# Attention scores as four 64x64 tiles in two PSUM banks, v windows copied by GpSimd, and a new split of PSUM banks

## The chip, the cores and the metric

The kernel runs on one NeuronCore of one Trainium2 chip. Its time is device microseconds (us) of one execution, and the comparison is between medians of several runs. PE is TensorE (PEld its weight loads), DVE is VectorE, ACT is ScalarE, POOL is GpSimd, and SP is the engine that issues most DMAs.

## What is computed

The reference is sliding-window attention over 64 keys, followed by two mixture-of-experts layers. The change touches only the attention:

```python
q, k, v: [4, 8, 576, 64] float32           # batch, heads, positions, head dim
scores = (1.0 / np.sqrt(64)) * np.matmul(q, k.transpose(0, 1, 3, 2))
rel = pos[:, None] - pos[None, :]
scores = np.where((rel >= 0) & (rel < 64), scores, -1000000000.0)
scores = scores - np.max(scores, axis=-1, keepdims=True)
attn = np.exp(scores)
attn = attn / (np.sum(attn, axis=-1, keepdims=True) + 1e-09)
out = np.matmul(attn, v)                   # then [2304, 512] tokens
x = _moe_ref(x=out, ...)                   # 8 experts, 288 tokens each
return _moe2_ref(x=x, ...)                 # 8 experts, argmax of a softmax
```

## The kernel before

The 2304 tokens are cut into 18 tiles `t` of 128 tokens. A tile holds two blocks of 64 queries (`bb` = 0, 1). A block needs 128 keys: its own 64 and the 64 before them. The 8 heads are worked on as two halves `hf` = 0, 1: the even heads lie on partitions 0 to 63 of the transposed q and k, the odd ones on 64 to 127.

For one tile the work runs as follows. `load_qk` and `load_v` bring q, k and v by DMA from SP. `tr` transposes k and q on TensorE into a PSUM tile `tr`, and VectorE or ScalarE copies them to `K1` and `qa`. `attn(t, hf)` writes a mask into the PSUM tile `S` by an identity matmul (L377) and adds the scores of four heads onto it (L380: for each head two matmuls of 64x64 weights, one for each block). VectorE takes the row maximum (`mx`, L387) and its negative multiple (`nb`, L388). ScalarE makes the exponentials `P` (L392). TensorE transposes `P` into the PSUM tile `PT` (L398), and VectorE or ScalarE copies that to `pt`. TensorE multiplies by v into the PSUM tile `PV` (L408; the 65th column of v is one, and gives the sum). `fin` normalizes on VectorE into `x` (`sm`, its reciprocal and a product: L442, L444, L445). Then `parts` splits x into two f16 halves `x16` (high part on ScalarE, VectorE or GpSimd; low part L415 on GpSimd), stores them to `xd` by DMA, and transposes them (`xT`, L429); they are copied to `xt`, and the gate's logits follow (L470, L472, reduced by VectorE into `LG`, L475).

The second matmul operand of PV is v of the window: `vs` is v of the tile, and `vw` has the first 64 rows of this tile and the last 64 rows of the tile before. `windows` fills `vw` by two DMAs a tile from SP (L344, L347).

A planner sets the order in which each engine's instructions stand (`_Order`): every step is added with its engine or engines, an assumed duration, the tiles that it reads and writes, and a priority; `emit` places steps in assumed time and issues them in that order. A tile with n buffers can be written again when the steps of n tiles before are done. PSUM has 8 banks, and the attention shares them as tr 1, xT 1, S 2, PT 2, PV 2:

```python
bufs = dict(lk=4, lq=4, vs=4, vw=4, tr=1, xT=1, qa=3, S=2, mx=4, nb=4, P=3, PT=2, pt=3,
            PV=2, sm=4, x=3, x16=3, xt=3, K=RS)
```

When the last tile's logits are there, the attention's buffers are given back, and only then do the loads of the expert weights (L183) and the routing begin; the experts' matmuls follow to the end of the program.

Of the kernel before, what the change touches and what calls it, by code (L numbers as in the profile page):

```python
# [21 lines left out]
BF = mybir.dt.bfloat16  # L22
I32 = mybir.dt.int32
AF = mybir.ActivationFunctionType
ALU = mybir.AluOpType
# [118 lines left out]
def attn_moe_moe(ctx: ExitStack, tc: tile.TileContext, q, k, v, w_gate, w1a, w2a, emb, tau, w1b, w2b, out, dbg=None):  # L144
    nc = tc.nc
    dbg = dbg or {}
    B, H, S, D = q.shape
# [65 lines left out]
    idb = consts.tile([128, 128], BF, name="idb")  # L213
# [45 lines left out]
    MV = -8.0e9  # L259
    pa = ExitStack()  # L260
    wk = pa.enter_context(tc.tile_pool(name="attn", bufs=2))
    ps = pa.enter_context(tc.tile_pool(name="attn_ps", bufs=2, space=PSUM))
    dk = wk.tile([128, 2, 64], I32, name="dk", bufs=1)
    for g in range(2):
        nc.gpsimd.iota(dk[64 * g:64 * g + 64], pattern=[[0, 2], [1, 64]], base=0, channel_multiplier=-1)
    mt = wk.tile([128, 2, 64], F32, name="mt", bufs=1)
    masks = [wk.tile([128, 4, 2, 64], BF, name=f"mask{i}", bufs=1) for i in range(3)]
    for bb in range(2):
        sl = slice(64 * bb, 64 * bb + 64)
        nc.vector.tensor_scalar(mt[sl, bb], dk[sl, bb], 0.0, MV, op0=ALU.is_gt, op1=ALU.mult)  # L270
        nc.vector.tensor_scalar(mt[sl, 1 - bb], dk[sl, 1 - bb], 0.0, MV, op0=ALU.is_le, op1=ALU.mult)
    for i in range(3):
        nc.vector.tensor_copy(masks[i], mt[:, None].to_broadcast([128, 4, 2, 64]))
    nc.vector.memset(masks[1][0:64, :, 1], MV)
    nc.vector.memset(masks[2][64:128, :, 0], MV)
    wgf = wk.tile([128, NC, E], F32, name="wgf", bufs=1)
    nc.scalar.dma_start(wgf, w_gate.rearrange("(c p) e -> p c e", p=128))
    wgc = wk.tile([128, NC, 2, E], F16, name="wgc", bufs=1)
# [3 lines left out]
    RS = 4  # L282
# [1 line left out]
    K1 = wk.tile([128, RS, 4, 2, 64], F32, name="K1", bufs=1)  # L284
    nc.gpsimd.memset(K1[:, RS - 1, :, 1], 0.0)

    bufs = dict(lk=4, lq=4, vs=4, vw=4, tr=1, xT=1, qa=3, S=2, mx=4, nb=4, P=3, PT=2, pt=3,
                PV=2, sm=4, x=3, x16=3, xt=3, K=RS)
    shapes = dict(lk=([128, 8, 64], F32), lq=([128, 8, 64], F32), vs=([128, 8, 65], F32),
                  vw=([128, 8, 65], F32), qa=([128, 4, 2, 64], F32), S=([128, 4, 128], F32),  # L290
                  mx=([128, 4], F32), nb=([128, 4], F32), P=([128, 4, 128], F32), PT=([128, 4, 128], F32),
# [10 lines left out]
    g = g_  # L302
# [7 lines left out]
    def win(h, te, to):  # L310
        a = K1[64 * (h % 2):64 * (h % 2) + 64, te, h // 2]
        ap = [list(z) for z in a.ap]
        ap[1][0] += (to - te) * 512
        return bass.AP(tensor=a.tensor, offset=a.offset, ap=ap)

    TK, LGS = {}, {}
# [24 lines left out]

    def windows(t):
        vs, vw = TK['vs', t], TK['vw', t]
        ls.dma(1.3, .46, lambda: nc.sync.dma_start(g(vw)[0:64], g(vs)[0:64]), (vs,), (vw,), 2 * t)  # L344
        if t + 1 < NT:
            vn = TK['vw', t + 1]
            ls.dma(1.3, .46, lambda: nc.sync.dma_start(g(vn)[64:128], g(vs)[64:128]), (vs,), (vn,), 2 * t + 1)  # L347

    def tr(t, nm, tag='tr'):
        x, p, pr = TK[nm, t], ls.slot(tag), 2 * t - 2  # L350

        def pf():
            return g(p) if tag in ('tr', 'xT') else g(p).rearrange("p a n -> p (a n)")

        def f():
            for n in range(4):
                nc.tensor.transpose(pf()[:, n * 128:(n + 1) * 128], g(x)[:, 2 * n:2 * n + 2].rearrange("p a d -> p (a d)"), idf)
        ls.add('PE', .52 if t else .9, f, (x,), (p,), pr)
        y = TK[nm.upper(), t] = ls.slot('K' if nm == 'k' else 'qa')

        def to():
            z = K1[:, t % RS] if nm == 'k' else g(y)
            return z.rearrange("p h o i -> p (h o i)")
        ls.add(('DVE', 'ACT'), (.68, .6), lambda e: copy(e, to(), pf()), (p,), (y,), pr)

    def attn(t, hf):
        pr = 2 * t + hf
        mk = masks[0]
        if t * 128 % S == 0:
            mk = masks[1]  # L370
        if (t * 128 + 64) % S == 0:
            mk = masks[2]
        p, qa = ls.slot('S'), TK['Q', t]
        te, tp = t % RS, (t - 1) % RS

        def f():
            nc.tensor.matmul(g(p), idb, mk, start=True, stop=True)  # L377
            for hh in range(4):
                for bb in range(2):
                    nc.tensor.matmul(g(p)[bb * 64:bb * 64 + 64, hh],  # L380
                                     g(qa)[64 * hf:64 * hf + 64, hh, bb],
                                     win(2 * hh + hf, te, te if bb else tp), start=False, stop=True,
                                     skip_group_check=True)
        kd = [TK['K', t]] + ([TK['K', t - 1]] if t else [])
        ls.add('PE', 1.2, f, [qa] + kd, (p,), pr)
        mx, nb, P = ls.slot('mx'), ls.slot('nb'), ls.slot('P')
        ls.add('DVE', .68, lambda: nc.vector.tensor_reduce(g(mx), g(p), axis=AX.X, op=ALU.max), (p,), (mx,), pr)  # L387
        ls.add('DVE', .15, lambda: nc.vector.tensor_scalar(g(nb), g(mx), -0.125, None, op0=ALU.mult), (mx,), (nb,), pr)  # L388
# [202 lines left out]
    for t in range(NT):  # L591
        if t + 3 < NT:
            loads(t + 3)
        windows(t)
        attn(t, 0)
        if t + 1 < NT:
            front(t + 1)
        attn(t, 1)
        fin(t)
        if t == 9:  # L600
            small()
        if t == NP:
            spread()
# [706 lines left out]
    for i in range(2):  # L1310
# [5 lines left out]
        def f(i=i, pf=pf):  # L1316
            for l in range(2):
                for c in range(NC):
                    nc.tensor.transpose(pf()[:, l, c], G2[0, i].bitcast(F16)[:, (l * NC + c) * 128:(l * NC + c + 1) * 128], idh)
# [197 lines left out]
```

## Time and profile before

| | |
|---|---|
| median of 3 runs | 677.07 us (674.95 to 679.09) |
| the profiled execution, its own time | 676.5 us |
| its span in the profile | 674.7 us |
| TensorE busy over the span | 615.6 us (91%) |
| VectorE, ScalarE, GpSimd busy | 387.1 us, 325.9 us, 158.5 us |
| mean granted TensorE clock | 0.97 |

The span is what the profiler saw of one execution; the execution's own time is 1.8 us longer. The busy times are sums over stages that have different limits: attention ends after about a fifth of the span, and the experts take the rest.

### The profile page before, as it was taken

What the parts mean: (1) busy time and instruction counts of PE and PEld (TensorE: products, weight loads), DVE (VectorE), ACT (ScalarE), POOL (GpSimd) and SP (SyncE); (2) the same over time, 40 slices, a digit from 0 to 9 for tenths busy, and PEclk for the clock granted to TensorE, in tenths of its full rate; (3) what the DMA queues carried; (4) which work ended last, traced back from release to release, by engine and by line L of the source; (5) the groups of instructions that cost most, each with busy time, mean ns of one, the idle gap of its engine ahead of it and who ended that gap; (6) DMA issues with size and microseconds to landing.
All of it is one profiled execution on the core that took longest, in us unless ns stands there. A gap on an engine that the chain in (4) does not pass through costs nothing. (4 is left out here: it accounts for less than half of the span.)

```text
span 674.7 us, 16654 instructions
## 1 busy us (share of the span) xinstructions
PE 615.6 (91%) x6626; PEld 461.5 (68%) x6644; DVE 387.1 (57%) x995; ACT 325.9 (48%) x626; POOL 158.5 (23%) x222
## 2 busy tenths in 40 slices
PE   7998999878689999999999997898999799899994
PEld 5876787633347887877877887585866577568671
DVE  4777777768702478788688785462656671152010
ACT  3655655556632356556456664362656562352110
POOL 1242122100141243242322110431322430312101
PEclk9999999969989999999999997998999899999997
DMA  9999784154427489999999673496579882132100
GB/s 194 210 238 209 190 203 106 48 204 168 144 61 208 83 243 236 271 276 252 249 279 213 217 247 102 129 365 229 154 279 352 302 307 75 59 104 65 38 22 23
DMA packets 135069, 124.06 MB, mean 184 GB/s; under 512 B 99095, under 2 KB 99223, under 8 KB 134946
## 3 DMA queue, kind: packets, MB, share of 16 engines
q1 hardware_dynamic: 126114, 102.24, 54.4%
q0 software_dynamic: 5616, 17.60, 8.7%
q10 hardware_dynamic: 3216, 2.64, 1.4%
q8 instruction: 69, 1.13, 0.7%
q14 instruction: 54, 0.44, 0.2%
HBM read 94.17 MB, written 14.64 MB: 161 GB/s over the span
## 5 line engine op out<-in xcount | busy, mean ns | idle before, releaser
L1380 PE MATMUL pp<-x,w1h 128*128 128x128 f16 (+1 forms) x1280 | 99.3, 215 | 3.3 <-issue 2.6
L1380 PE MATMUL pp<-x,w1l 128*128 128x128 f16 (+1 forms) x640 | 98.1, 215 | 0.0
L1019 PE MATMUL pp<-xt,w1h 128*128 128x288 f16 x512 | 96.4, 289 | 1.7 <-ACT xt L999 1.7
L1034 PE MATMUL pp<-h,w2h 128*128 128x288 f16 x512 | 94.7, 286 | 0.0
L1380 PEld LDWEIGHTS <-w1h 128*128 128x128 f16 x1280 | 90.6, 100 | 4.4 <-issue 3.0
L1393 PEld LDWEIGHTS <-h 128*128 128x128 f16 (+1 forms) x480 | 47.3, 101 | 53.2 <-issue 1.7
L193 ACT ACTIVATE w2h<-wst 128x1024 f16<-128x1024 f32 x64 | 66.9, 1052 | 17.2 <-DMA wst<-in_moe_w_dram 16.9
L196 DVE SCALAR_TENSOR_TENSOR w2l<-wst,w2h 128x1024 f16<-128x1024 f32 x56 | 67.6, 1219 | 11.3 <-ACT w2h L193 9.9
L1019 PE MATMUL pp<-xt,w1l 128*128 128x288 f16 x256 | 74.0, 289 | 0.0
L1034 PE MATMUL pp<-h,w2l 128*128 128x288 f16 x256 | 73.2, 286 | 0.0
L193 ACT ACTIVATE w1h<-wst 128x1024 f16<-128x1024 f32 x64 | 66.6, 1051 | 13.4 <-DMA wst<-in_moe_w_dram 13.2
L196 DVE SCALAR_TENSOR_TENSOR w1l<-wst,w1h 128x1024 f16<-128x1024 f32 x56 | 67.3, 1214 | 3.3 <-ACT w1h L193 3.1
L1384 DVE SCALAR_TENSOR_TENSOR h<-pp,h 128x512 f16<-128x512 f32 (+1 forms) x40 | 24.8, 620 | 69.8 <-ACT h L1383 69.8
L1380 PEld LDWEIGHTS <-w1l 128*128 128x128 f16 x640 | 62.3, 100 | 0.7 <-issue 0.7
L1019 PEld LDWEIGHTS <-w1h 128*128 128x128 f16 x512 | 49.7, 99 | 14.3 <-issue 1.8
L1034 PEld LDWEIGHTS <-w2h 128*128 128x128 f16 x512 | 49.8, 98 | 12.3
L1393 PE MATMUL pp<-w2h,h 128*128 128x512 f16 (+1 forms) x192 | 57.2, 379 | 0.0
L1397 POOL DMA_INDIRECT out_dram<-o,xg x20 | 19.9, 997 | 147.7 <-ACT o L1396 113.1
L1022 ACT ACTIVATE h<-pp 128x288 f16<-128x288 f32 x64 | 26.2, 409 | 43.9 <-PE pp L1019 41.0
L392 ACT ACTIVATE P<-S,nb 128x128 f32<-128x128 f32 x144 | 41.0, 374 | 11.5 <-DVE sm L444 4.3
L380 PE MATMUL S<-K,qa 64*64 64x128 f32 x576 | 41.4, 285 | 4.9 <-issue 1.8
L1383 ACT ACTIVATE h<-pp 128x512 f16<-128x512 f32 (+1 forms) x40 | 21.7, 542 | 49.5 <-PE pp L1380 44.3
(289 smaller groups left out, 1173.4 us busy)
## 6 DMA issues: line engine op xcount, KB each, us to landing
wst<-in_moe_w_dram SPq DMA_DIRECT2D x124, 512.0 KB, 5.9
yd<-yr SPq DMA_DIRECT2D x8, 578.2 KB, 6.2
xd<-x SPq DMA_DIRECT2D x18, 256.0 KB, 3.1
vw<-vs SPq DMA_DIRECT2D x35, 130.0 KB, 3.8
lk<-in_k_dram SPq DMA_DIRECT2D x16, 256.0 KB, 4.0
lq<-in_q_dram SPq DMA_DIRECT2D x16, 256.0 KB, 4.5
vs<-in_v_dram SPq DMA_DIRECT2D x16, 256.0 KB, 4.9
wst<-in_moe_w_dram ACTq DMA_DIRECT2D x4, 512.0 KB, 5.6
```

Source lines behind the costliest of these rows:

```text
L193: nc.scalar.activation(w_slice(key, i, 0), ST[key, i], AF.Copy, scale=32.0)
L196: nc.vector.scalar_tensor_tensor(w_slice(key, i, 1), ST[key, i], 32.0, w_slice(key, i, 0), op0=ALU.mult, op1=ALU.subtract)
L380: nc.tensor.matmul(g(p)[bb * 64:bb * 64 + 64, hh], g(qa)[64 * hf:64 * hf + 64, hh, bb], win(2 * hh + hf, te, te if bb else tp), start=Fals ...
L392: nc.scalar.activation(g(P)[:, hh], g(p)[:, hh], AF.Exp, bias=g(nb)[:, hh:hh + 1], scale=0.125)
L1019: nc.tensor.matmul(g(p)[:, :CAP], w1s(key, i, c, f_), g(xt)[:, j, c], start=(n == 0), stop=(n == 11))
L1022: ls.add('ACT', .29, lambda f_=f_, p=p: nc.scalar.activation(g(h[f_])[:, 0], g(p)[:, :CAP], AF.Relu), (p,), (h[f_],), 20 * e)
L1034: nc.tensor.matmul(g(p)[:, :CAP], w2s(key, i, f_, d * 128, 128), g(h[f_])[:, j], start=(f_ == 0 and n == 0), stop=(f_ == NF - 1 and n == 2))
L1380: nc.tensor.matmul(p[:, i], w1s(key, w, c, 4 * fg + i), xt[:, l, c, :n], start=(k == 0), stop=(k == 11))
L1383: nc.scalar.activation(hh[:, 0], p, AF.Relu)
L1384: nc.vector.scalar_tensor_tensor(hh[:, 1], p, 0.0, hh[:, 0], op0=ALU.max, op1=ALU.subtract)
L1393: nc.tensor.matmul(po[:m], h[:, l, f_, :m], w2s(key, w, f_), start=(k == 0), stop=(k == 23))
L1397: nc.gpsimd.indirect_dma_start(out=out, out_offset=bass.IndirectOffsetOnAxis(ap=xr.bitcast(I32)[:m, DM:DM + 1], axis=0), in_=o[:m], in_off ...
```

## The change

The scores of both halves of a tile become one step, `scores(t)`. It takes two `S` tiles (two banks) at once. Masks are now written as four 64x64 tiles too (block by half), and the scores' matmuls go in the order head, block, half, so that four matmuls in a row use four different quarters of the array. The mask constants become one set for each block. The copies into `vw` move from SP's DMAs to `tensor_copy` on GpSimd, with a priority one step earlier. The transposes of k and q get an earlier priority. The PSUM shares become tr 2, xT 1, S 3, PT 1, PV 1.

```diff
+    masks = [[wk.tile([128, 4, 2, 64], BF, name=f"mask{bb}{i}", bufs=1) for i in range(2)] for bb in range(2)]
+    nc.vector.tensor_scalar(mt[:, 0], dk[:, 0], 0.0, MV, op0=ALU.is_gt, op1=ALU.mult)
+    nc.vector.tensor_scalar(mt[:, 1], dk[:, 1], 0.0, MV, op0=ALU.is_le, op1=ALU.mult)
     for bb in range(2):
...
+        for i in range(2):
+            for o in range(2):
+                if o != bb and i:
+                    nc.gpsimd.memset(masks[bb][i][:, :, o], MV)
+                else:
+                    nc.vector.tensor_copy(masks[bb][i][:, :, o], mt[:, None, int(o != bb)].to_broadcast([128, 4, 64]))
...
-    bufs = dict(lk=4, lq=4, vs=4, vw=4, tr=1, xT=1, qa=3, S=2, mx=4, nb=4, P=3, PT=2, pt=3,
-                PV=2, sm=4, x=3, x16=3, xt=3, K=RS)
+    bufs = dict(lk=4, lq=4, vs=4, vw=4, tr=2, xT=1, qa=3, S=3, mx=4, nb=4, P=3, PT=1, pt=3,
+                PV=1, sm=4, x=3, x16=3, xt=3, K=RS)
...
-        ls.dma(1.3, .46, lambda: nc.sync.dma_start(g(vw)[0:64], g(vs)[0:64]), (vs,), (vw,), 2 * t)
+        ls.add('POOL', .6, lambda: nc.gpsimd.tensor_copy(g(vw)[0:64], g(vs)[0:64]), (vs,), (vw,), 2 * t - 1)
...
-            ls.dma(1.3, .46, lambda: nc.sync.dma_start(g(vn)[64:128], g(vs)[64:128]), (vs,), (vn,), 2 * t + 1)
+            ls.add('POOL', .6, lambda: nc.gpsimd.tensor_copy(g(vn)[64:128], g(vs)[64:128]), (vs,), (vn,), 2 * t)
...
-        x, p, pr = TK[nm, t], ls.slot(tag), 2 * t - 2
+        x, p, pr = TK[nm, t], ls.slot(tag), 2 * t - 4
...
+    def scores(t):
+
+        mk = [masks[0][t * 128 % S == 0], masks[1][(t * 128 + 64) % S == 0]]
+        p2, qa = [ls.slot('S') for _ in range(2)], TK['Q', t]
+        te, tp = t % RS, (t - 1) % RS
+        TK['S', t] = p2
+
+        def f():
+            for bb in range(2):
+                for hf in range(2):
+                    z = slice(64 * hf, 64 * hf + 64)
+                    nc.tensor.matmul(g(p2[hf])[bb * 64:bb * 64 + 64], idb[z, z], mk[bb][z], start=True, stop=True)
+            for hh in range(4):
+                for bb in range(2):
+                    for hf in range(2):
+                        nc.tensor.matmul(g(p2[hf])[bb * 64:bb * 64 + 64, hh],
+                                         g(qa)[64 * hf:64 * hf + 64, hh, bb],
+                                         win(2 * hh + hf, te, te if bb else tp), start=False, stop=True,
+                                         skip_group_check=True)
+        kd = [TK['K', t]] + ([TK['K', t - 1]] if t else [])
+        ls.add('PE', 1.4, f, [qa] + kd, p2, 2 * t)
+
     def attn(t, hf):
         pr = 2 * t + hf
...
-        p, qa = ls.slot('S'), TK['Q', t]
...
-            nc.tensor.matmul(g(p), idb, mk, start=True, stop=True)
...
-        ls.add('PE', 1.2, f, [qa] + kd, (p,), pr)
+        p = TK['S', t][hf]
```

On TensorE, in the middle of the attention of the kernel before, each half's scores stand by themselves between other steps (`S` the scores, `PT` the transposed exponentials, `tr` the transposes of k and q):

```order
L377 LDWEIGHTS idb
L377 MATMUL S<-mask_122,idb 128x512
L380 MATMUL S<-K_139,qa 64x128 x8
L398 MATMUL PT<-idf,P 128x128 x4
L357 MATMUL tr<-idf,lq 128x128 x4
```

One mask of 128x128 and eight score matmuls make one half; the other half of the tile follows later, with its own mask.

On TensorE of the changed kernel, at the scores of tile 5, whose two halves are `S_754` and `S_756` (`PT_744` is the first half of tile 4, and the numbers name buffers):

```order
L405 MATMUL PT_744<-idf_72,P_708 128x128 x4
L379 LDWEIGHTS idb_74
L379 MATMUL S_754<-mask00_122,idb_74 64x512
...
L379 MATMUL S_756<-mask00_122,idb_74 64x512
...
L379 MATMUL S_754<-mask10_124,idb_74 64x512
...
L379 MATMUL S_756<-mask10_124,idb_74 64x512
L383 MATMUL S_754<-K1_141,qa_625 64x128
L383 MATMUL S_756<-K1_141,qa_625 64x128
L383 MATMUL S_754<-K1_141,qa_625 64x128
```

Two masks and two groups of scores at two places have become one group at one place, with halves in turn; 16 score matmuls of this kind stand together, and the other steps of tile 4 follow behind them.

On VectorE of the changed kernel, from the scores of tile 5 on (`PV_798` and `PV_857` are the two halves of tile 4, one PSUM bank after the other):

```order
L394 TENSOR_REDUCE mx_809<-S_754 128x4
L449 TENSOR_SCALAR sm_817<-PV_798 128x4
L395 TENSOR_SCALAR nb_824<-mx_809 128x4
L451 RECIPROCAL sm_817<-sm_817 128x4
L394 TENSOR_REDUCE mx_829<-S_756 128x4
L452 TENSOR_TENSOR x_854<-PV_798,sm_817 128x4x64
L310 COPY K1_141<-tr_819 128x512
L310 COPY xt_879<-xT_845 128x1024
L449 TENSOR_SCALAR sm_905<-PV_857 128x4
L395 TENSOR_SCALAR nb_907<-mx_829 128x4
L451 RECIPROCAL sm_905<-sm_905 128x4
L452 TENSOR_TENSOR x_854<-PV_857,sm_905 128x4x64
```

The maximum of the second half stands between the reciprocal and the product that frees the only `PV` bank, and two copies stand ahead of the second half's normalization.

On GpSimd of the kernel before, in the same part of the program (`vs` gets its column of ones by a memset, and L415 makes the low part of x):

```order
L339 MEMSET vs_544 128x8
L308 CAST x16_581<-x_523 128x512
L415 TENSOR_TENSOR x16_581<-x_523,x16_581 128x512
L339 MEMSET vs_722 128x8
L415 TENSOR_TENSOR x16_753<-x_685,x16_753 128x512
```

GpSimd has a short memset and the splitting of x here, and nothing that waits for the load of v.

On GpSimd of the changed kernel, in the same part:

```order
L346 COPY vw_610<-vs_491 64x520
L349 COPY vw_737<-vs_491 64x520
L341 MEMSET vs_751 128x8
L346 COPY vw_737<-vs_618 64x520
L422 TENSOR_TENSOR x16_787<-x_713,x16_787 128x512
L349 COPY vw_843<-vs_618 64x520
```

The copies of v of tile 6 (`vs_618`) now stand ahead of the low part of x of tile 3, so that this low part waits for a load of v three tiles later than its own.

## Rows read from the trace of the kernel before

**Rows 1.** Busy time of each engine (and number of instructions), steady attention, by windows.

```profile
core 0: us, PE busy (x) PEld busy (x) DVE busy (x) ACT busy (x) POOL busy (x), PEclk, DMA share, GB/s
60.00:100.00 40.00, 37.59 (x577) 31.62 (x579) 29.10 (x89) 22.14 (x65) 7.62 (x12) 1.00 0.84 194
```

**Rows 2.** Timeline of TensorE: start, duration, instruction; two tiles' distance at the end.

```profile
61.70 0.18 PE L470 MATMUL xT<-wgc,xt 128*128 128x16 f16 x1
...
61.92 0.64 PE L398 MATMUL PT<-idf,P 128*128 128x128 f32 x4
62.39 0.60 PE L357 MATMUL tr<-idf,lq 128*128 128x128 f32 x4
63.24 0.27 PE L408 MATMUL PV<-vw,pt 128*64 128x65 f32 x1 [0.25 <-ACT pt L306]
...
63.86 0.39 PE L377 MATMUL S<-mask,idb 128*128 128x512 bf16 x1
64.18 1.09 PE L380 MATMUL S<-K,qa 64*64 64x128 f32 x16
65.20 0.62 PE L429 MATMUL xT<-idh,x 128*128 128x128 f16 x8
65.66 0.61 PE L398 MATMUL PT<-idf,P 128*128 128x128 f32 x4
...
77.75 1.09 PE L380 MATMUL S<-K,qa 64*64 64x128 f32 x16
```

**Rows 3.** The same timeline, cut after 0.13 and 0.23 us of one scores group.

```profile
64.18 0.33 PE L380 MATMUL S<-K,qa 64*64 64x128 f32 x2
...
64.18 0.44 PE L380 MATMUL S<-K,qa 64*64 64x128 f32 x4
```

**Rows 4.** VectorE by line and form, 60 to 100 us: count, busy, mean ns, idle before.

```profile
L387 DVE TENSOR_REDUCE mx<-S 128x4 f32<-128x512 f32 x12 | 8.3, 689 | 7.3 <-PE S L380 7.3
...
L388 DVE TENSOR_SCALAR nb<-mx 128x4 f32<-128x4 f32 x12 | 2.5, 204 | 0.2
```

**Rows 5.** Timelines of GpSimd and VectorE: one nb beside a GpSimd step, one alone.

```profile
75.80 1.16 POOL L415 TENSOR_TENSOR x<-x,x 128x512 f16<-128x512 f32 x1 [1.61 <-ACT x L306]
...
76.55 0.43 DVE L388 TENSOR_SCALAR nb<-mx 128x4 f32<-128x4 f32 x1
80.10 0.16 DVE L388 TENSOR_SCALAR nb<-mx 128x4 f32<-128x4 f32 x1
```

**Rows 6.** GpSimd by line and form, attention: the nearest rows to a copy.

```profile
L308 POOL CAST x<-x 128x512 f16<-128x512 f32 x2 | 1.2, 612 | 5.2 <-DVE sg L567 4.2 <-DVE x L445 1.0
...
L330 POOL MEMSET vw<- 64x520 f32 x1 | 0.5, 526 | 0.1
```

**Rows 7.** DMA from 60 to 100 us: packets; issues with KB and us to landing.

```profile
DMA packets 20209, 7.75 MB, mean 194 GB/s; under 512 B 18740, under 2 KB 18740, under 8 KB 20203
...
vw<-vs SPq DMA_DIRECT2D x12, 130.0 KB, 3.7
...
vs<-in_v_dram SPq DMA_DIRECT2D x5, 256.0 KB, 4.8
```

**Rows 8.** Timeline: scores of tile 2, last scores, first weight load behind the attention.

```profile
20.07 1.09 PE L380 MATMUL S<-K,qa 64*64 64x128 f32 x16 [0.25 <-ACT qa L306]
...
127.19 1.09 PE L380 MATMUL S<-K,qa 64*64 64x128 f32 x16
...
137.55 1.87 SPq L183 DMA_DIRECT2D wst<-in_moe_w_dram  x4
```

**Rows 9.** Timeline of ScalarE and VectorE in one half: copy of PT, exponentials, normalization.

```profile
62.59 0.60 ACT L306 ACTIVATE pt<-PT 128x512 f32<-128x512 f32 x1 [1.93 <-PE PT L398]
63.60 1.14 ACT L392 ACTIVATE P<-S,nb 128x128 f32<-128x128 f32 x4
...
63.97 0.16 DVE L442 TENSOR_SCALAR sm<-PV 128x4 f32<-128x4 f32 x1
...
64.38 0.42 DVE L445 TENSOR_TENSOR x<-PV,sm 128x256 f32<-128x256 f32 x1
```

More of the change, by code (lines that the diff above doesn't have):

```diff
@@ L266, in attn_moe_moe @@
     mt = wk.tile([128, 2, 64], F32, name="mt", bufs=1)
-    masks = [wk.tile([128, 4, 2, 64], BF, name=f"mask{i}", bufs=1) for i in range(3)]
+    masks = [[wk.tile([128, 4, 2, 64], BF, name=f"mask{bb}{i}", bufs=1) for i in range(2)] for bb in range(2)]
+    nc.vector.tensor_scalar(mt[:, 0], dk[:, 0], 0.0, MV, op0=ALU.is_gt, op1=ALU.mult)
+    nc.vector.tensor_scalar(mt[:, 1], dk[:, 1], 0.0, MV, op0=ALU.is_le, op1=ALU.mult)
     for bb in range(2):
[L269 to L275, printed above, removed]
+        for i in range(2):
[4 more added lines that the diff above has]
+                    nc.vector.tensor_copy(masks[bb][i][:, :, o], mt[:, None, int(o != bb)].to_broadcast([128, 4, 64]))
     wgf = wk.tile([128, NC, E], F32, name="wgf", bufs=1)
@@ L364, in tr @@
         ls.add(('DVE', 'ACT'), (.68, .6), lambda e: copy(e, to(), pf()), (p,), (y,), pr)
+    def scores(t):
[17 more added lines that the diff above has]
+        ls.add('PE', 1.4, f, [qa] + kd, p2, 2 * t)
     def attn(t, hf):
         pr = 2 * t + hf
[L368 to L372, printed above, removed]
-        p, qa = ls.slot('S'), TK['Q', t]
-        te, tp = t % RS, (t - 1) % RS
-        def f():
-            nc.tensor.matmul(g(p), idb, mk, start=True, stop=True)
[L378 to L384, printed above, removed]
-        ls.add('PE', 1.2, f, [qa] + kd, (p,), pr)
+        p = TK['S', t][hf]
         mx, nb, P = ls.slot('mx'), ls.slot('nb'), ls.slot('P')
@@ L594, in attn_moe_moe @@
         windows(t)
+        scores(t)
         attn(t, 0)
```

## The prediction, made before the changed kernel was run

> **What bounds the kernel now.** I read the attention alone, since the change ends there: the first weight load stands at 137.55 us, directly behind it, and nothing of the experts starts earlier [rows 8]. So time saved in the attention should shorten the program by as much. First the busy time by windows: from 60 to 100 us TensorE is busy 37.59 of 40 us, VectorE 29.10, ScalarE 22.14, GpSimd 7.62, all at the full clock [rows 1]. Then what VectorE waits for: its largest idle time is 7.3 us ahead of the row maximum, and TensorE's scores end it [rows 4]. So TensorE sets the pace. Its timeline gives a tile's time: the scores at 64.18 and 77.75 us are the same half, two tiles apart, so a tile takes 13.57 / 2 = 6.79 us [rows 2].
>
> From one start to the next, the timeline prices TensorE's steps [rows 2]: mask 0.32 (63.86 to 64.18), scores of a half 1.02 (to 65.20), transposes of x 0.46 (to 65.66), a group of four transposes 0.47 (61.92 to 62.39), gate 0.22 (61.70 to 61.92), PV 0.62 (63.24 to 63.86). A tile has two masks and two scores (2.68), four groups of transposes (1.88), two PV (1.24), x (0.46), gate (0.22): 6.48 us. So TensorE really waits only 0.31 us a tile.
>
> **The change on TensorE.** Cut 0.13 us after its start, a scores group has two rows, and 0.10 us later four; each pair adds 0.11 us [rows 3]. A float32 matmul has two rows here (16 rows for eight matmuls), so two column tiles work at the same time, in eight steps of about 0.107 us (0.86), and 0.16 us pass before the next step. No row shows two row halves of the array at work together. If they do, 32 rows in fours need the same eight steps: both halves cost 1.02, and the four mask tiles go side by side like one mask, 0.32. That is 1.34 in place of 2.68, a gain of 1.34 us a tile. If they don't, the scores need 16 steps, 1.88; the masks are two in sequence. The transposes of x stream 8 x 128 f16 columns in 0.46 [rows 2], so 512 columns take 0.23, and two masks 0.55: 2.43 in all, a gain of 0.25. I take the first: the pairs already overlap fully between column halves, and the halves of the new order write two different banks. TensorE then needs 6.48 - 1.34 = 5.14 us a tile.
>
> **VectorE next.** It is busy 29.10 / 40 x 6.79 = 4.94 us a tile [rows 1]. The reductions, nb and normalizations stay; of the copies that may run on it or ScalarE (K, q, pt, xt, high part of x) the new plan gives VectorE 45 over the 18 tiles in place of 48, which I cost at nothing: at some 0.6 us each it is 0.1 us a tile. ScalarE had 22.14 / 40 x 6.79 = 3.76 us and takes no more. So VectorE, covered until now, becomes as long as TensorE.
>
> **The copies of v.** Two leave SP's queue for GpSimd in each tile. No row shows a float32 copy on GpSimd; a cast of 128x512 took 0.61 and a memset of 64x520 0.53 [rows 6]. I take 0.61, since it also reads; 0.53 and the 1.16 of the two-input L415 [rows 5] are the bounds. GpSimd goes from 1.29 to about 2.6 us a tile (four more casts of x over the whole attention included), with room in any tile time of 5 us. But VectorE feels it: the nb at 76.55 us took 0.43 instead of 0.16, and ended at 76.98, just as GpSimd's step of 75.80 did (76.96) [rows 5]. On average nb took 0.204 [rows 4], 0.044 above the undisturbed row, with GpSimd busy 19% of the time. At 2.6 / 5.6 = 46% it becomes some 0.11, that is 0.13 us more a tile for two. At most two nb and a cast each wait half a copy, three times 0.3. I take 0.2: VectorE 5.14, level with TensorE.
>
> The Trainium skill (SBUF — State Buffer, Who interferes with whom) says that VectorE and GpSimd share one pair of SBUF ports under an exclusive lock, and that the second to start is blocked for the whole instruction of the first. The two rows above agree. By that rule alone, with each of the 36 nb held for a whole copy, the loss would be 36 x 0.61 = 22 us, more than the change gains; by the measured mean it is 2 to 4 us.
>
> On GpSimd a copy now waits for a load of v three tiles ahead, and behind it stand the low part of x, then the transposes of x on TensorE. The load can start once PV has freed its buffer, two tile times less about 1.1 us ahead of those transposes: 10 us at 5.6 a tile. Issue 0.6, landing 4.8 [rows 7], copy 0.61 and L415 1.16 [rows 5, 6] are 7.2. So 2.8 us of cover hide it; without them TensorE would wait for the excess in each tile.
>
> **DMA.** Twelve window copies of 130 KB are 1.56 of 7.75 MB from 60 to 100 us [rows 7], a fifth; at a DMA share of 0.84 [rows 1] a tile's DMA work was 5.7 us and falls to about 4.6 by bytes. Nothing waited on it much before; it stays hidden under a tile of 5.6. If none of it fell, 5.7 a tile would be the floor.
>
> **One bank for PT and PV.** The first half's bank must now be emptied before the second half is written. For PV the order gives VectorE sm 0.16, nb 0.20, reciprocal 0.18, a maximum 0.69 and the product 0.42, 1.65 us [rows 4, 5, 9] (the reciprocal is what fits between the two rows of VectorE in the last of these), while TensorE has PT, two transposes of k and q and those of x in between, 1.87. On the way to the next tile, two copies of about 0.69 and a normalization (0.96) take 2.3 us against 2.03 (PT, the new scores, gate): short by 0.3. For PT a copy of 0.60 behind four exponentials of 1.14 [rows 9] is 1.74 against about 2.0. So I count 0.3 of wait here.
>
> **The sum.** 5.14 plus this 0.3 and half of the old wait (0.15) make 5.6 us a tile; the bounds are 5.3 (waits almost gone) and 6.15 (1.0 of wait, the mutual waiting of two engines that are both full). From the scores of tile 2 to the last ones, 20.07 to 127.19 us [rows 8], are 107.1 / 6.79 = 15.8 tile times, so the gain is 15.8 x 1.19 = 18.8. The last scores now bring two halves at once, and one more maximum and set of exponentials (0.69 + 1.14) follow behind them: minus 1.8. The cold first tiles and the mask constants I take as even. The profiled execution took 676.5 us, 0.6 below the median of the runs; 676.5 - 17 = 659.5, say 660. With the two bounds it is 655 to 668.
>
> **Rivals.** *Row halves don't work together*: gain 0.25 a tile, 15.8 x 0.25 = 4, less the 1.8 at the end, so 674. For it: no row here shows them at once. Against it: the column halves do so without loss. *GpSimd's lock*: both nb and the cast are held each time by 0.3 and more, VectorE needs about 5.9, TensorE waits for it, and a tile takes about 6.2: 15.8 x 0.59 - 1.8 = 7.5 gained, 669. For it: the rows at 75.80 and 76.55. Against: most nb rows were short. The rule of the Trainium skill (SBUF — State Buffer, Who interferes with whom) is this rival. *Single banks decide*: each of the four handovers a tile (two PT, two PV) is late. This loses as soon as TensorE waits over 6.79 - 5.14 = 1.65 us a tile, 0.41 at each; at 0.5 each a tile takes 7.14, and the program 676.5 + 15.8 x 0.35 + 1.8 = 684. For it: one of the four is short already by my own count, and both emptying engines get fuller. Against: three are covered by 0.2 to 0.3 us. *The gain has no way out*: DMA or the load-copy-L415 path holds a tile at 6.7, 675; against it stands the fifth of DMA work that goes.
>
> **Chances.** Forecast (5.3 to 6.1 a tile) 0.63, waits vanish and TensorE alone decides (5.14 a tile, 652) 0.06, row halves in sequence 0.07, lock 0.10, single banks 0.08, no way out 0.06. A change of under 0.5% (3.4 us) can't be told from none. Forecast, vanished waits and lock are faster: 0.79; row halves in sequence and no way out are the same: 0.13; slower 0.08. The range leaves out single banks, no way out and about half of the vanished waits: 652 to 674.
>
> **What would show it.** In the profile after, the scores of a tile should be one group of 32 rows in about 1.1 us busy with rows in fours; if it takes 1.9, the first rival holds. The tile distance of scores should be near 5.6, VectorE busy above 90% in the middle, its wait for scores nearly gone, nb's mean near 0.27, a GpSimd copy near 0.6, and the first weight load at about 120.5 us. TensorE waiting on sm or pt ahead of PV and PT by over 0.4 us each would show single banks; GpSimd waiting on v's load with TensorE idle ahead of the transposes of x would show the load path. The prediction is wrong if the first weight load comes early and the end does not follow.

## The result, and the profile after

The changed kernel takes 659.2 us (median of 4 runs, 657.16 to 662.07), the kernel before 676.86 us (median of 4, 674.95 to 679.09): a ratio of 0.974, 95% interval 0.969 to 0.979. It is faster by 17.7 us; 660 was predicted. The profiled execution of after took 662.07 us, the slowest of its four, with a span of 660.3.

In the profile the whole gain lies in the attention. The first weight load, which stood at 137.55 us [rows 8], and the last product `x` of the normalization (134.79 us before) now read as follows; SPq is SP's DMA queue, the first number is the start, the second the duration, and `xN` counts rows drawn together:

```profile
120.32 0.41 DVE L452 TENSOR_TENSOR x<-PV,sm 128x256 f32<-128x256 f32 x1
123.07 1.87 SPq L183 DMA_DIRECT2D wst<-in_moe_w_dram  x4
```

Both are 14.5 us earlier; the end of the execution is 14.4 us earlier (676.5 to 662.07). From the first weight load to the end of the span it is 537.2 us in both profiles. In the profiles of the experiments below whose experts run on the same data, that stretch takes 532.2 to 543.0 us, though nothing in it was changed. I therefore compare stages by landmarks inside the attention, and totals by ratios.

Busy time from 60 to 100 us, to be held against [rows 1] (columns as there):

```profile
60.00:100.00 40.00, 36.53 (x688) 31.46 (x684) 35.39 (x105) 26.12 (x75) 20.09 (x36) 1.00 0.56 141
```

TensorE is nearly as full as before (36.53 us, after 37.59), but VectorE has gone from 29.10 to 35.39 and GpSimd from 7.62 to 20.09, and the DMA share has fallen from 0.84 to 0.56. TensorE's timeline of a tile, against [rows 2]:

```profile
62.78 0.66 PE L405 MATMUL PT<-idf,P 128*128 128x128 f32 x4
63.37 0.41 PE L379 MATMUL S<-mask,idb 64*64 64x512 bf16 x4
63.61 1.04 PE L383 MATMUL S<-K,qa 64*64 64x128 f32 x32
64.58 0.18 PE L477 MATMUL xT<-wgc,xt 128*128 128x16 f16 x1
...
66.85 0.61 PE L436 MATMUL xT<-idh,x 128*128 128x128 f16 x8
67.91 0.24 PE L415 MATMUL PV<-vw,pt 128*64 128x65 f32 x1 [0.45 <-DVE nb L395]
```

All 32 score rows of a tile take 1.04 us, less than the 16 rows of one half took before (1.09); the four masks need 0.24. Masks and scores of a tile cost 63.37 to 64.58, 1.21 us, where [rows 2] gave 2.68. At 67.91 TensorE has waited 0.45 us, by the profile's account for VectorE's `nb`. Cut short, the group shows how many rows have started or run by a given moment:

```profile
63.61 0.39 PE L383 MATMUL S<-K,qa 64*64 64x128 f32 x8
63.61 0.61 PE L383 MATMUL S<-K,qa 64*64 64x128 f32 x16
63.61 0.82 PE L383 MATMUL S<-K,qa 64*64 64x128 f32 x24
```

Eight rows come every 0.22 us, where a group of before ([rows 3] cut it too) has two every 0.11: four tiles of the array work at once.

VectorE's and GpSimd's groups from 60 to 100 us and over the attention (busy, mean ns of one, then idle time ahead):

```profile
L394 DVE TENSOR_REDUCE mx<-S 128x4 f32<-128x512 f32 x15 | 10.0, 675 | 1.4 <-PE S L383 1.2
L395 DVE TENSOR_SCALAR nb<-mx 128x4 f32<-128x4 f32 x15 | 7.2, 480 | 0.2
...
L346 POOL COPY vw<-vs 64x520 f32<-64x520 f32 x18 | 11.3, 626 | 27.0 <-DMA vs<-in_v_dram 22.7 <-PE PT L405 2.9 <-ACT pt L308 1.1
L349 POOL COPY vw<-vs 64x520 f32<-64x520 f32 x17 | 10.6, 622 | 1.8 <-DMA vs<-in_v_dram 0.9
```

VectorE's wait for scores, 7.3 us in [rows 4], is 1.4, and it is busy 88% of the time. `nb`, four values a partition in and four out, takes 480 ns on average where it took 204 (over the whole attention 355, where it took 225). The longest one shows why:

```profile
83.31 0.62 POOL L346 COPY vw<-vs 64x520 f32<-64x520 f32 x1
83.89 1.15 POOL L422 TENSOR_TENSOR x<-x,x 128x512 f16<-128x512 f32 x1
```
```profile
83.60 1.47 DVE L395 TENSOR_SCALAR nb<-mx 128x4 f32<-128x4 f32 x1
```
```profile
85.19 1.14 ACT L399 ACTIVATE P<-S,nb 128x128 f32<-128x128 f32 x4 [1.98 <-DVE sm L451]
```

The `nb` at 83.60 ends at 85.07, 0.03 us after GpSimd's subtraction (85.04), which follows a copy directly; ScalarE's exponentials start only then. This is [rows 5] again, but through two GpSimd instructions in a row. The Trainium skill (SBUF — State Buffer, Who interferes with whom) gives the rule, an exclusive lock between the two engines on a shared pair of ports, and the trace agrees that the second one waits until the first is done. That the hold is the lock and not something else is not separated here.

Which GpSimd instruction holds `nb` can be read off as well. Of the 36 `nb` rows of the changed kernel 23 take at most 0.17 us; each of the 13 others (0.30 us and more) ends 0.02 to 0.03 us behind a GpSimd instruction. From 60 to 100 us seven of 15 are held, six of them to the end of the subtraction, one (78.17) to the end of a copy. One of the six:

```profile
71.23 1.16 POOL L422 TENSOR_TENSOR x<-x,x 128x512 f16<-128x512 f32 x1
```
```profile
71.46 0.95 DVE L395 TENSOR_SCALAR nb<-mx 128x4 f32<-128x4 f32 x1
```

The kernel before has the same subtraction, and there two `nb` of 12 were held by it (76.55 and 90.19). So what `nb` waits for is mostly the subtraction, not a copy. The copies still matter, since the subtraction stands behind them on GpSimd: with the copies taken from GpSimd and the order kept, `nb` takes 297 ns (e6) or 334 (e10), between 204 and 480.

The load path was named in the prediction and priced at nothing; once it cost a stall. These are GpSimd, TensorE, and then the windows (us; busy of PE, PEld, DVE, ACT, POOL; clock; DMA share; GB/s) around 42 us:

```profile
41.00 0.61 POOL L346 COPY vw<-vs 64x520 f32<-64x520 f32 x1 [3.66 <-DMA vs<-in_v_dram]
41.58 1.14 POOL L422 TENSOR_TENSOR x<-x,x 128x512 f16<-128x512 f32 x1
```
```profile
42.77 0.40 PE L436 MATMUL xT<-idh,x 128*128 128x128 f16 x4 [3.31 <-POOL x L422]
```
```profile
38.00:40.00 2.00, 1.46 (x16) 1.27 (x14) 1.79 (x6) 1.60 (x6) 0.00 (x0) 1.00 1.17 237
40.00:42.00 2.00, 0.00 (x0) 0.00 (x0) 0.00 (x0) 0.52 (x2) 1.00 (x2) 1.00 0.85 206
42.00:44.00 2.00, 1.23 (x20) 1.12 (x20) 0.69 (x1) 0.00 (x0) 1.33 (x2) 0.80 1.05 231
44.00:46.00 2.00, 2.00 (x20) 1.37 (x20) 1.26 (x5) 0.74 (x2) 1.39 (x3) 0.50 1.18 286
```

A load of v comes late; GpSimd's copy waits for it, the subtraction behind the copy with it, and TensorE's transposes of x 3.31 us. The load is that of tile 6, which takes the buffer that tile 2 had (`vs` has four). The last PV of tile 2 on TensorE, and the load on SP's queue:

```profile
28.23 0.27 PE L415 MATMUL PV<-vw,pt 128*64 128x65 f32 x1
```
```profile
34.89 0.66 SPq L339 DMA_DIRECT2D vs<-in_v_dram  x1
```

The load lands 6.06 us after 34.89. But SP comes to it only some 6 us after the buffer is free: from 26.3 to 41.2 us its issues (v of tile 5 takes 2.02 us, the next k 2.33) follow each other with at most 0.1 us between them. After the idle stretch the granted clock is down to 0.80 and then 0.50, the lower level.

**Landmarks.** The 36 products `x` (one for each half tile, numbered from 0) mark the attention's progress. I use number 11, number 31 (ten tiles later) and number 35, the last. Each row of the table is one profiled execution. In the kernel before and after they are:

```profile
56.50 0.41 DVE L445 TENSOR_TENSOR x<-PV,sm 128x256 f32<-128x256 f32 x1
124.62 0.41 DVE L445 TENSOR_TENSOR x<-PV,sm 128x256 f32<-128x256 f32 x1
134.79 0.41 DVE L445 TENSOR_TENSOR x<-PV,sm 128x256 f32<-128x256 f32 x1
```
```profile
52.49 0.41 DVE L452 TENSOR_TENSOR x<-PV,sm 128x256 f32<-128x256 f32 x1
111.72 0.42 DVE L452 TENSOR_TENSOR x<-PV,sm 128x256 f32<-128x256 f32 x1
```

| kernel | number 11 at | to number 31, per tile | 31 to 35 | last at | ratio to before (95%) |
|---|---|---|---|---|---|
| before | 56.50 | 6.81 | 10.17 | 134.79 | |
| after | 52.49 | 5.92 | 8.60 | 120.32 | 0.974 (0.969 to 0.979) |
| e1 halves apart | 50.25 | 6.27 | 8.60 | 121.57 | 0.978 (0.972 to 0.984) |
| e2 no nb | 52.66 | 5.67 | 10.56 | 119.89 | 0.971 (0.965 to 0.977) |
| e3 before, no nb | 56.76 | 6.81 | 10.18 | 135.06 | 1.004 (1.000 to 1.007) |
| e4 before, copies alone | 55.75 | 6.82 | 10.17 | 134.09 | 0.997 (0.993 to 1.000) |
| e5 old matmuls | 57.16 | 7.13 | 8.48 | 136.93 | 1.002 (0.999 to 1.005) |
| e6 windows by DMA | 52.86 | 6.38 | 10.67 | 127.28 | 0.988 (0.983 to 0.994) |
| e8 no q loads | 49.23 | 5.22 | 9.44 | 110.86 | (other data) |
| e9 no q DMA | 45.57 | 5.93 | 10.60 | 115.43 | (other data) |
| e10 copies on ScalarE | 50.05 | 6.09 | 10.62 | 121.59 | 0.975 (0.968 to 0.981) |
| e11 no nb, copies on ScalarE | 49.73 | 5.90 | 8.48 | 117.25 | 0.973 (0.967 to 0.978) |
| e12 old masks | 49.25 | 6.09 | 8.48 | 118.61 | 0.980 (0.972 to 0.987) |

The gain of 14.5 us is 4.0 up to number 11, 8.9 in the ten tiles, and 1.6 at the end. The kernel before has a stall of its own ahead of number 11, in which VectorE waits for `em`, a small load for the routing; after has none there (`em` is issued at 44.63 us, before at 48.51):

```profile
52.63 0.68 DVE L541 SCALAR_TENSOR_TENSOR en<-em 8x512 f32<-8x512 f32 x1 [3.21 <-DMA em<-in_moe_expert_emb_dram]
```

The stretch from 31 to 35 has two lengths in the profiles of the changed kernel and its variants: 8.48 to 8.60 us at a granted clock of 1.00, and 10.56 to 10.67 (e2, e6, e9, e10) at 0.68 to 0.69, with e8 between them; why the clock falls there in some is not shown. The kernel before ran beside each group of experiments, at 675.16 us (e1 to e4), 681.25 (e5 to e8) and 682.04 (e9 to e12); so the ratios tell more than absolute times. e7 has no row here, since its profiled execution was one of three slow ones of its ten; the time in its section is the median of the other seven.

### The profile page after: what moved, and what is told of

Same layout as the page of the kernel before. It is cut to its first block, busy times and chain, and to the rows that moved or that the text cites. A ratio compares the mean times of both kernels' runs of the same rounds, so it can differ in the third digit from the quotient of the medians.

```text
span 660.3 us, 16725 instructions
## 1 busy us (share of the span) xinstructions
PE 596.3 (90%) x6680; PEld 446.2 (68%) x6680; DVE 386.3 (59%) x991; ACT 324.3 (49%) x625; POOL 182.7 (28%) x263
## 5 line engine op out<-in xcount | busy, mean ns | idle before, releaser
L1027 PEld LDWEIGHTS <-w1h 128*128 128x128 f16 x512 | 49.7, 99 | 14.4 <-issue 1.8
L1142 POOL TENSOR_TENSOR z<-yr 96x512 f32<-96x512 f16 x18 | 23.2, 1291 | 77.6 <-DMA yr<-yl 55.8
```

The source lines that it names most:

```text
L1027: nc.tensor.matmul(g(p)[:, :CAP], w1s(key, i, c, f_), g(xt)[:, j, c], start=(n == 0), stop=(n == 11))
L1142: ls.add('POOL', 1.1, lambda j=j, z=z: nc.gpsimd.tensor_tensor(g(z), yrv(yr)[:MT, j, :DM], yrv(yr)[:MT, j, DM:2 * DM], op=ALU.add), (yr,), ...
```

## The experiments

**Does the gain come from the four tiles at once?** e1 issues the same small matmuls half by half:

```diff
-            for bb in range(2):
-                for hf in range(2):
+            for hf in range(2):
+                for bb in range(2):
...
-            for hh in range(4):
-                for bb in range(2):
-                    for hf in range(2):
+            for hf in range(2):
+                for hh in range(4):
+                    for bb in range(2):
```

> The changed kernel with its masks and scores issued first for all even heads and then for all odd ones, so that a row half never has work while the other has; all else as changed. If the gain comes from both row halves working at once: the group of 32 score rows takes 1.8 to 2.1 us where it took 1.04, the four mask rows up to 0.8 where they took 0.41, the steady distance of two tiles grows from 5.98 by 0.4 to 1.1 us (VectorE is nearly as full as TensorE and hides a part), and the time is 666 to 674 us. If the order in banks and halves does nothing and the gain is that of the copies, the PSUM shares and the earlier transposes: 657 to 661 us, with score groups still near 1.04.

It took 659.63 us, a ratio of 0.978: no loss that the totals can tell, so the expectation missed. TensorE's timeline, and the score group cut at four moments, show why:

```profile
62.40 0.41 PE L379 MATMUL S<-mask,idb 64*64 64x512 bf16 x4
62.63 1.54 PE L383 MATMUL S<-K,qa 64*64 64x128 f32 x32
...
62.63 0.38 PE L383 MATMUL S<-K,qa 64*64 64x128 f32 x4
62.63 0.60 PE L383 MATMUL S<-K,qa 64*64 64x128 f32 x8
62.63 1.10 PE L383 MATMUL S<-K,qa 64*64 64x128 f32 x24
62.63 1.32 PE L383 MATMUL S<-K,qa 64*64 64x128 f32 x28
```

Four rows per 0.22 us at both ends, but 16 rows in the 0.50 us between: the odd rows start while the even ones still run. So e1 takes away about half of the overlap (1.54 in place of 1.04), and the ten tiles are 0.35 us longer each. It did not have the stall at 42 us, which gives 2.2 us back by number 11; in all the last product is 1.25 us later. That test did not decide, so e5 puts the matmuls of before, a 128x128 mask and 16 rows for each half, in the place of the new ones, with all else as changed:

```diff
+            for hf in range(2):
+                nc.tensor.matmul(g(p2[hf]), idb, mk, start=True, stop=True)
+                for hh in range(4):
+                    for bb in range(2):
...
```

> The changed kernel with the matmuls of before in the place of the new ones: for the even heads and then for the odd ones one mask row of 128x128 and 16 score rows, no row half ahead of the other; the copies on GpSimd, the PSUM shares, the earlier transposes and the order stay as changed. From the rows before, mask and scores of one half take 0.32 + 1.02 us, so 2.68 a tile, where the changed kernel takes 1.21 (63.37 to 64.58) and the one with halves apart 1.71 (62.40 to 64.11; its odd rows start while the even ones still run). If TensorE's shorter tile is the gain: TensorE needs 5.4 + 1.5 = 6.9 us a tile, the distance of two tiles is 6.6 to 6.9, and the time 670 to 677 us. If the rest of the change (copies, shares, earlier transposes) brings half of it: 662 to 668 us.

The ratio is 1.002: the whole gain is gone, and a tile takes 7.13 us, longer than before and than the 6.6 to 6.9 expected. TensorE's own time is as expected (38.57 / 40 x 7.13 = 6.87 a tile), so it stands at the head again; `nb` is at 225 ns:

```profile
60.00:100.00 40.00, 38.57 (x564) 32.39 (x570) 28.11 (x90) 24.10 (x68) 19.87 (x42) 1.00 0.59 141
```

GpSimd's copies are all there (19.87 busy), so they hold `nb` little at this pace and order. On TensorE the halves stay apart (the first mask row of the group is not in the trace):

```profile
29.48 1.09 PE L383 MATMUL S<-K,qa 64*64 64x128 f32 x16
30.50 0.39 PE L380 MATMUL S<-mask,idb 128*128 128x512 bf16 x1
30.82 1.09 PE L383 MATMUL S<-K,qa 64*64 64x128 f32 x16
```

e12 brings back only the two 128x128 masks, ahead of the new 32 rows.

> The changed kernel with the two 128x128 mask rows of before and the 32 score rows in turn of the change. It leaves TensorE 0.4 us a tile more (two masks 0.64, four small ones 0.24). Theory: TensorE and VectorE are nearly equal, so the steady tile grows from 5.92 by 0.1 to 0.4 us and the time by 2 to 6 us, to 660 to 664. Rival (row halves need masks of their own to work at once, so a score group takes 2.0 as with the old matmuls): 675 us or more. Rival (VectorE alone sets the tile): 657 to 660 us.

A ratio of 0.980 and 6.09 us a tile: 0.17 more a tile for TensorE's 0.35 (from the first mask to the step behind the scores 1.56 at 103.71, the only such group behind the first with both mask rows in the trace, where after takes 1.21). The score group stays at 1.10, so the halves don't need masks of their own to work at once:

```profile
72.39 0.38 PE L380 MATMUL S<-mask,idb 128*128 128x512 bf16 x1
72.70 1.10 PE L384 MATMUL S<-K,qa 64*64 64x128 f32 x32
```

**Do the other parts bring anything alone?** e4 is the kernel before with the copies on GpSimd (the two lines of `windows`), e7 the kernel before with the new PSUM shares.

> The kernel before with one part of the change alone: the shifted tiles of v copied by GpSimd, where SP's DMAs copied them. Theory: TensorE still sets the tile of 6.79 us; nb lengthens from 0.20 to 0.3 to 0.5 us and lies in VectorE's idle time; the DMA share falls from 0.84 to about 0.6 without a use: 673 to 679 us. Rival (the DMAs taken away are what gives the gain): 660 to 670 us. Second rival (the copies alone lose, by the held nb and the copies' own wait for their load): 680 us or more.

> The kernel before with the PSUM shares of the change alone: two banks for the transposes of q and k and three for S, one each for PT and PV. Theory: TensorE's tile of 6.48 us still sets the time; with one bank each for PT and PV it waits for the engines that empty them by up to 0.3 us a tile, and gets up to that back at the transposes: 674 to 682 us. Rival (single banks decide, a loss that the changed kernel hides): 685 us or more. Rival (the third S bank is a gain by itself): 670 us or less.

e4: 673.14 us, 0.997 (0.993 to 1.000), 6.82 us a tile, `nb` 235 ns, DMA share 0.63 to 0.68 in the slices from 40 to 100 us. e7: 679.06 us, 0.996 (0.992 to 1.001). Neither can be told from no change. The new scores alone in the kernel before, and the earlier transposes alone, were not run, so whether the new matmuls would bring the gain without the other parts is not shown.

**What does the hold on nb cost?** e2 removes `nb` from the changed kernel, e3 from the kernel before, in the same way:

```diff
-        ls.add('DVE', .68, lambda: nc.vector.tensor_reduce(g(mx), g(p), axis=AX.X, op=ALU.max), (p,), (mx,), pr)
-        ls.add('DVE', .15, lambda: nc.vector.tensor_scalar(g(nb), g(mx), -0.125, None, op0=ALU.mult), (mx,), (nb,), pr)
+        ls.add('DVE', .68, lambda: nc.vector.tensor_reduce(g(nb), g(p), axis=AX.X, op=ALU.max, negate=True), (p,), (mx, nb), pr)
+        ls.add('DVE', .15, lambda: None, (mx,), (nb,), pr)
...
-                nc.scalar.activation(g(P)[:, hh], g(p)[:, hh], AF.Exp, bias=g(nb)[:, hh:hh + 1], scale=0.125)
+                nc.scalar.activation(g(P)[:, hh], g(p)[:, hh], AF.Exp, bias=g(nb)[:, hh:hh + 1])
```

> The changed kernel without the 36 VectorE instructions nb = -0.125 mx: the copy of the transposed q scales by 0.125, the reduction writes the negated maximum, and the exponential takes it as its bias. The order of all other instructions stays. Theory (VectorE, lengthened where nb waits for GpSimd's copies and subtractions, sets the distance of two tiles): 0.48 us twice a tile leave VectorE, the steady distance falls from 5.98 to 5.3 to 5.6, the time to 648 to 655 us. Rival (TensorE with its 36.5 busy of 40 us sets it, and what nb waits for costs nothing): 657 to 661 us. Second rival (what counts is the one step less between score and exponential, not VectorE's load): the same gain as below in the kernel before.

> The kernel before without nb, in the same way. Theory: TensorE sets its tile of 6.79 us, VectorE has idle time there, and nb takes 0.20 there: no change, 673 to 678 us. If one step less between score and exponential is what counts, it gains as much as the changed kernel does without nb, 4 to 9 us.

Without `nb` the ten tiles of the changed kernel take 5.67 us each, 0.25 less, but not the 5.3 to 5.6 expected; the kernel before gains nothing (1.004). So one step less between score and exponential is not what counts; `nb` costs where VectorE is full. But the last four products took 10.56 us, 2 more than in after, at the lower clock named above. The windows of e2 and of after, in this order:

```profile
110.00:120.00 10.00, 7.72 (x102) 6.52 (x102) 5.18 (x18) 2.20 (x5) 2.74 (x3) 0.69 0.15 54
```
```profile
110.00:120.00 10.00, 7.25 (x130) 6.26 (x130) 6.15 (x22) 3.45 (x8) 2.93 (x3) 1.00 0.15 55
```

The total, 0.971, overlaps that of after. e10 keeps `nb` and gives the copies to ScalarE instead, e11 does both:

```diff
-        ls.add('POOL', .6, lambda: nc.gpsimd.tensor_copy(g(vw)[0:64], g(vs)[0:64]), (vs,), (vw,), 2 * t - 1)
+        ls.add('POOL', .6, lambda: nc.scalar.activation(g(vw)[0:64], g(vs)[0:64], AF.Copy), (vs,), (vw,), 2 * t - 1)
```

> The changed kernel with the two copies of v a tile on ScalarE, in the same place of the order; GpSimd keeps only its subtractions and small memsets. Theory (GpSimd's copies hold nb, and VectorE sets the steady tile): nb from 0.48 to 0.25 to 0.35 us, ScalarE from 3.9 to 5.1 busy us a tile, still under the tile of 5.92, which falls to 5.6; 652 to 657 us. Rival (ScalarE now waits for the loads of v with the exponentials behind it in its queue, and TensorE for them): 660 to 668 us. Both at once: no change, 657 to 660 us.

> Both edits that keep GpSimd and VectorE apart: no nb (the maximum is written negated, q is scaled as it is copied) and the copies of v on ScalarE. If the steady tile is still VectorE's and GpSimd's matter: 5.3 to 5.6 us a tile, 648 to 654 us. If without nb nothing is left that GpSimd's copies hold: no better than without nb alone, ratio to before 0.97; if ScalarE's waits for the loads of v decide: 658 us or more.

With the copies on ScalarE `nb` takes 334 ns, and not 204:

```profile
60.00:100.00 40.00, 35.58 (x670) 29.90 (x667) 32.76 (x102) 34.29 (x89) 10.08 (x18) 1.00 0.50 129
```
```profile
L395 DVE TENSOR_SCALAR nb<-mx 128x4 f32<-128x4 f32 x14 | 4.7, 334 | 0.2
```

The subtraction of x16, which GpSimd had before as well, still holds it. ScalarE is the fullest engine but TensorE now (34.29), and a tile takes 6.09, 0.17 more than on GpSimd, not the 5.6 of the theory. e11 has 5.90. Neither total can be told from that of after. So of the variants tried, e2 has the lowest ratio, but none is shown to beat the changed kernel.

**What do the DMA engines cost?** e6 issues the copies as SP's DMAs at the same place of the order (`nc.sync.dma_start` for `nc.gpsimd.tensor_copy`).

> The changed kernel with the shifted tiles of v copied by SP's DMAs again, issued where GpSimd's copies stood in the order. nb should fall from 0.48 to 0.2 to 0.35 us (only the subtraction of x16 is left to wait for). Theory A (GpSimd's hold on nb is what the copies cost): 648 to 655 us. Theory B (until the loads are through, at some 45 to 80 us, the DMA engines are nearly full, share 0.9, and 0.27 MB more a tile make each of the first tiles 0.5 to 1.3 us longer, which eats what nb gives): 657 to 668 us, with the tile of scores number 8 (start 52.33 now) at 55 to 60. Theory C (the copies wait on SP's queue behind other transfers, and TensorE for them): over 668 us.

`nb` falls to 297 ns, but the ratio is 0.988, and the ten tiles take 6.38 each:

```profile
40.00:60.00 20.00, 16.10 (x299) 13.98 (x295) 12.77 (x43) 11.62 (x35) 7.04 (x35) 0.96 0.99 232
60.00:80.00 20.00, 19.65 (x329) 17.33 (x330) 14.82 (x52) 13.22 (x39) 6.83 (x21) 0.87 1.03 225
```

The DMA engines are full until 80 us (share 0.99 and 1.03), but the extra time is not spread over the tiles. Nearly all of it lies in one wait, for `em`, which SP issues at 54.93 us here, behind two copies, and at 44.63 in after:

```profile
54.93 0.52 SPq L542 DMA_DIRECT2D em<-in_moe_expert_emb_dram  x1
57.51 0.68 DVE L548 SCALAR_TENSOR_TENSOR en<-em 8x512 f32<-8x512 f32 x1 [4.24 <-DMA em<-in_moe_expert_emb_dram]
60.22 0.34 PE L415 MATMUL PV<-vw,pt 128*64 128x65 f32 x1 [3.79 <-DVE nb L395]
```

VectorE waits 4.24 us, TensorE 3.79 behind it, and from 60 to 65 us the granted clock is 0.50. Behind it, from product 14 (68.12, in after 61.61) to 31, a tile takes 5.70, in after 5.90. Early on there is one wait of TensorE for a copy itself, 4.70 us ahead of 19.62. The sign of theory B is missing: the eighth group of scores starts at 52.83 (52.33 in after), not at 55 to 60. The early wait is that of theory C, the later one of its kind, a load late on SP's queue. Whether SP's order or the full DMA engines make `em` late is not separated. So the whole change is better with the copies off SP's queue (0.974 against 0.988, intervals apart), though they cost up to 0.2 us a tile where nothing waits for a load; alone they gain nothing that can be told (e4).

e8 and e9 leave out q's loads. In e8 the planner knows it, so the order changes too; in e9 the steps stay in the plan, and the order is that of the changed kernel:

```diff
-        ls.dma(len(_segs(t * 128, 128, S)), 1.17, f, (), (x,), 2 * t - 7)
+        ls.dma(len(_segs(t * 128, 128, S)), 1.17, f if nm == 'k' else (lambda: None), (), (x,), 2 * t - 7)
```

> The changed kernel without the loads of q, with k's rows in the place of q's for the transposes; so what is computed is the attention of k with itself, and a quarter of the DMA work of each tile is left out; every other instruction stays. If the DMA engines hold back the first eight tiles (share 0.9 between 20 and 45 us, and the wait for the load of v before 41.00): score groups start without the gap of 9.76 us between 35.83 and 45.59, the eighth starts at 47 to 49 in place of 52.33, and the time is 652 to 657 us. If not: 658 to 661 us.

> The changed kernel with its order kept and only q's DMAs left out (k's rows are transposed twice, so the output is another attention, and what comes after the attention runs on other data: read the attention's end, not the whole time). The last product x of the attention starts at 120.32 us now, the half tile number 11 at 52.49. If the DMA engines hold the tiles back, by late loads of v and k: half tile 11 at 48 to 50, 5.2 to 5.6 us a tile behind it where it is 5.92, the last x at 111 to 116. If the gain of the run without q loads came from the other order that it had: the last x at 119 to 121.

In both the stretch behind the attention runs on other data, and the whole time (729.27 and 730.18 us) says nothing here. In e9 product 11 stands at 45.57, 6.9 us earlier than in after and earlier than the 48 to 50 expected, with no gap; behind it a tile takes 5.93, as in after (5.92), not 5.2 to 5.6. So q's loads, in SP's queue and on the DMA engines, cost up to 6.9 us in the first six tiles and nothing in the ten that follow. The windows of e9 and e8 from product 11 to 31:

```profile
45.57:104.83 59.26, 53.23 (x1024) 45.38 (x1016) 49.50 (x153) 39.48 (x117) 29.68 (x60) 1.00 0.42 109
```
```profile
49.23:101.42 52.19, 48.27 (x939) 41.50 (x937) 43.09 (x138) 37.47 (x108) 27.16 (x48) 1.00 0.44 118
```

In e8 the eighth group of scores starts at 46.14, a little ahead of the 47 to 49 expected. Its 5.22 us a tile can't be held against the other rows as it stands: in its order only nine groups of scores lie between the two products, in e9 ten, and TensorE has 939 instructions there in place of 1024. For the work of one tile (a tenth of 1024) e8 needs 52.19 / 9.39 x 1.024 = 5.7 us, where e9 needs 5.93, at nearly the same DMA share. So the other order may be worth 0.2 to 0.3 us a tile. Which of its moves does it was not tried.

## Why the prediction held, point by point

- **TensorE's 1.34 a tile.** Right in mechanism and nearly in size: 2.68 became 1.21, so 1.47, since the small masks also take less (0.24 for 0.32). e5 shows that without it the gain is gone (that it is enough by itself is not shown); the rival of row halves in sequence is out, by the rows in eights.
- **The tile of 5.6 us.** Measured 5.92, within the bounds of 5.3 to 6.15. TensorE's waits were counted at 0.45 and are 0.5 (3.5 us ahead of PV in 6.8 tiles). The term that was too small is TensorE's own 5.14: by the window it is 36.53 / 40 x 5.92 = 5.4, although masks and scores came out lower than priced. Part of it is that a step which nothing follows at once counts in full: the transposes of x ahead of the wait at 67.91 take 0.61, where I had 0.46 to the next step. The rest I can't itemize.
- **The lock at 0.2 a tile.** Too small: `nb` alone grew from 204 to 480 ns, 0.55 for two. I had scaled the excess over the undisturbed row by GpSimd's busy share, and took half a copy as what an `nb` waits for at most. The rows show waits for the subtraction, which the kernel before had too, in six of seven cases (up to 0.95 us), and at 83.60 for a copy and the subtraction behind it. With the copies off GpSimd (e10) the mean is still 334 ns, so the new order has a part in it. That VectorE still came out near the forecast (35.39 / 40 x 5.92 = 5.24 for 5.14) is due to another term, costed at nothing: its copies and casts from PSUM and of x fell in this stretch from 1.97 us a tile (11.6 us in 5.9 tiles) to 1.72 (11.6 in 6.8). The lock rival (VectorE 5.9, a tile of 6.2) went too far: without any `nb`, 0.96 us a tile less on VectorE, the tile shrinks by 0.25 (e2).
- **What sets 5.92.** No engine alone. TensorE's additions of 0.35, 0.50 and 1.47 us lengthen the tile by 0.17, 0.35 and 1.21 (e12, e1, e5), so part is hidden each time, and the order of e8 does a tile's work in 5.7. How much such an order would give to the changed kernel itself stays open.
- **The load path, "2.8 us of cover hide it".** Wrong once. The copy at 41.00 waited 3.66 us for its load and TensorE 3.31 behind it, and the clock fell. Four runs without a gap of this size (e1, e10, e11, e12) have number 11 at 49.25 to 50.25, so it cost after some 2 to 3 us. The price of the path was nearly right: landing 6.06, copy 0.61 and subtraction 1.14 are 7.8, where 7.2 was forecast. The cover was wrong: I had the load start 10 us ahead of the transposes, as soon as its buffer is free; it started at 34.89, 4.6 us ahead of 39.46, where TensorE's wait begins, since SP came to it 6 us after the buffer was free. Why SP's issues ahead of it took so long (2.02 and 2.33 us) is not shown.
- **Copies at 0.61.** 0.608 and 0.614 us at the least, 0.63 and 0.62 on average: right. That fewer DMAs would stay without effect was right for e4 and wrong for the changed kernel (e6), there by two waits for late loads and not by a longer tile between them.
- **Single banks.** e7 has no loss that can be told from none, and in the changed kernel TensorE's waits from 60 to 100 us, all ahead of PV, sum to 3.5 us, where the rival needs 0.41 at each of four handovers in 6.8 tiles, 11 us. This rival is out.
- **The end, minus 1.8.** By the landmarks of that step it is minus 7.0: the last scores moved by 21.4 us (127.19 to 105.74) and the weight load by 14.5. The scores run further ahead now: when the last ones start, seven products are still to come (number 29 is at 105.82), before it were three. By products the last four half tiles are 1.6 us faster (8.60 against 10.17).
- **The sum.** 18.8 - 1.8 = 17.0 was forecast, 14.5 measured between the two profiled executions, and 17.7 between the medians. In the ten tiles 8.9 us came of 11.9 forecast (ten times 1.19). That the median came within 1 us of 660 owes something to the scatter of the part that was not changed.

## What to carry to other kernels

Shortening the engine that sets the pace gives back what the next ones allow: here 1.47 us of TensorE gave 0.89 a tile, with VectorE, the order and, early on, the loads close behind. Price a shared resource by the events of a row, not by a mean share: what matters is whether the small instruction falls behind a long one, and whether a second long one follows. For a load, ask when the queue that issues it will come to it, and not only how long it takes to land. Before a per-tile time between two landmarks is compared, count the work between them. And judge a small edit by landmarks inside its stage when the rest of the program scatters by more than the edit is worth.

## What I had not expected of the hardware

Matmuls issued half by half still overlapped: in e1 the odd half's rows, on the other 64 partitions and in another bank, started while the even half's still ran (16 rows in 0.50 us in the middle, four in 0.22 at the ends). In e5, where a 128x128 mask stands between the halves, each group of 16 rows takes its full 1.09 us. And after a stall of a few microseconds the clock's dip comes on top: TensorE idle from 40 to 42 us, granted clock 0.80 and 0.50 in the four microseconds behind it.
